# Agent attention with a mixture of experts: 140 stores issued by GpSimd instead of SyncE

## The chip, the cores and the metric

The kernel runs on one core of a Trainium2 chip. The metric is the device time of one execution in microseconds (us); lower is better. The engines of the core are named as the profile names them: PE is TensorE (matrix products; PEld are its weight loads), DVE is VectorE, ACT is ScalarE, POOL is GpSimd, and SP is SyncE, which computes nothing here and only issues DMAs. SPq and POOLq are the instruction queues of SP and POOL.

## The reference

Queries, keys and values are 4 x 11456 x 128, with 49 agents for each of the 4 batches. The agents attend to the keys and gather values; the queries then attend to the 49 agents; the result goes through a top-1 mixture of 8 experts with an inner width of 1024.

```python
def reference(q, k, v, agents, w_gate, w1, w2):
    a2k = softmax(scale * agents @ k.T)          # 49 x 11456 in each batch
    agent_v = a2k @ v                            # 49 x 128
    x = softmax(scale * q @ agents.T) @ agent_v  # 11456 x 128 in each batch
    x = x.reshape(45824, 128)
    logits = x @ w_gate                          # 8 experts
    e = argmax(logits); gate = softmax(logits)[e]
    out = gate * (relu(x @ w1[e]) @ w2[e])
```

## The kernel before

A batch of 11456 tokens is cut into 12 chunks: 11 of 1024 tokens (128 partitions x 8 tokens) and a remainder of 192 (96 x 2). In each batch one expert is applied densely to all tokens, and its product with `agent_v` is folded into the first layer, so that the first layer takes the 49 softmax numerators of a token instead of `x`. Tokens that belong to other experts are gathered, computed in 14 blocks of 128 and written over the dense result at the end, after about 1060 us.

**The dense part** (`experts`) sets the beat. A chunk has two groups of four 128-token tiles (`groups`, 23 in a batch), and a group has 8 steps, one for each 128 columns of the inner width: 184 steps in a batch. In a step TensorE makes two products of 128x512 from the transposed numerators `M` (lines 1186 and 1187), ACT applies the ReLU and rounds to the high half `hh` (line 1192), DVE makes the low half (line 1193), and five steps later (`LAG`) TensorE makes 12 products into `py` (line 1206). After the eighth step `store(g)` multiplies `py` by the gate on DVE into `yo` (line 1219; 3 buffers) and two steps later (`DST`) the 256 KB block goes to `out`.

**Beside it** the attention of the next batch and the rest of this batch's query chunks run, chunk by chunk: load `ld` (SP, line 286), sum of squares (ACT, line 330), split into two 16-bit halves `hl` (ACT line 362, DVE line 364), a DMA transpose to `hT` (SP, line 386, and 390 for the remainder), scores on TensorE (lines 414 to 416). A key chunk then gives `S` (ACT, line 432), later an exponential (ACT, line 481), a running sum `es` (mostly GpSimd, line 491) and products with the values. A query chunk gives `E` (DVE, line 595, subtracts the maximum), `qexp` takes the exponential (ACT, line 600) and stores it to `exps`, a scratch array in device memory, from which the leftover blocks later gather. `esplit` rounds `E` to 16 bits (DVE, line 607) and makes the low part (line 611; on GpSimd for the odd chunks of batches 0 to 2, 18 of 48, else on DVE), `eturn` transposes both to `M` (SP, line 617), and the logits follow on TensorE (line 626). In between, SP loads the experts' weights `wn` (line 905) into the buffers of the keys' `hT`, and ACT takes their sums of squares (line 910).

**The order** of the instructions is written by an event heap: `at(t, f)` puts a function at a step, `after(dt, f)` puts it `dt` steps behind the present one, and a loop at the end takes them out in order of time. A scheduler of the framework may still move instructions on an engine by its own rules when the kernel is built. Each engine then works its list strictly in order, and a DMA is an instruction in the list of the engine that issues it. The stores of the exponentials (48) and of the output (92) are events, and the trace files both under line 1282, from which the loop calls them.

GpSimd's other work: line 491, line 611, the ranks of the leftover tokens (lines 822 to 839), the indirect gathers of the leftover blocks (`fg` and `fx`, line 223) and their indirect stores at the end (line 1088).

## Time and profile before

| what | value |
|---|---|
| median of 3 runs | 1185.75 us (1181.12 to 1194.63) |
| profiled execution | 1183.18 us, of which the span of the instructions is 1181.5 us |
| TensorE busy | 1041.8 us, 88% |
| VectorE busy | 1000.6 us, 85% |
| ScalarE busy | 766.2 us, 65% |
| GpSimd busy | 142.9 us, 12% |
| DMA queues | 62.2% of the 16 engines' span for the queue that SP feeds, 1.1% for the one that GpSimd feeds |

Busy time counts computing instructions, and for GpSimd also the time in which it writes an indirect DMA's work list; it does not count the time in which SP issues a DMA. A share near 90% says that little is left to gain on an engine, and not which wait ends last at a given place; the lists of waits and the order of time say that.

### The profile page before, as it was taken

Reading aid. Unit: us, or ns where it says so; the run is one execution under the profiler, and the core shown is the slowest. Engines: PE = TensorE matmul, PEld = TensorE weight load, DVE = VectorE, ACT = ScalarE, POOL = GpSimd, SP = SyncE. Lnnn points to the kernel's source line nnn. Section 1 sums busy time; section 2 is a strip of 40 time slices with the busy share of each in tenths; the row PEclk is TensorE's granted clock in tenths of the full one; section 3 lists DMA queues with packets and bytes.
Section 4 is the critical chain, followed back from the end, with each engine's and each line's share of the span. In section 5 each row is a group of like instructions: output and inputs, shape, how many; then the busy total and the mean of one; then the engine's idle time right before and its main releaser. Section 6 shows DMA issues by size and latency. Waiting matters only on the chain.

```text
span 1181.5 us, 35109 instructions
## 1 busy us (share of the span) xinstructions
PE 1041.8 (88%) x14308; PEld 828.6 (70%) x14308; DVE 1000.6 (85%) x2512; ACT 766.2 (65%) x1362; POOL 142.9 (12%) x193
## 2 busy tenths in 40 slices
PE   6746989899998899899988989799989889999995
PEld 5625777677775777677776777677767667677885
DVE  7868989697788899698788999697789798899985
ACT  8547876574486786574485887574576556666682
POOL 0200000043000000042100000042000112110123
PEclk9759999999999999899998999999999999899998
DMA  8599899741299899741298899631365545433270
GB/s 325 183 244 222 190 206 232 182 112 46 81 267 222 166 244 219 193 122 40 101 253 224 192 227 215 165 101 49 109 165 117 116 102 132 127 100 125 64 272 14
DMA packets 265669, 190.98 MB, mean 162 GB/s; under 512 B 217513, under 2 KB 230306, under 8 KB 265504
## 3 DMA queue, kind: packets, MB, share of 16 engines
q1 hardware_dynamic: 263648, 185.39, 62.2%
q0 software_dynamic: 1568, 2.25, 1.1%
q8 instruction: 113, 1.85, 0.7%
q10 hardware_dynamic: 288, 1.05, 0.3%
q14 instruction: 52, 0.43, 0.1%
HBM read 99.75 MB, written 36.43 MB: 115 GB/s over the span
## 4 chain that ended last, share of the span: by engine, by line
PE 23%; DVE 16%; DMA 8%; issue 6%; ACT 5%; POOL 2%; SPq 0%; POOLq 0%; ACTq 0%; DVEq 0%
PE py L1206 11%; DVE hh L1193 7%; PE ph L1186 4%; PE ph L1187 4%; DMA M<-mm 3%; ACT hh L1192 2%; DMA wn<-in_moe_w_dram 2%; DVE S L476 1%; POOL out_dram L1088 1%; DMA ld<-in_q_dram 1%; DMA hT<-hl 1%; PE ps_small L504 1%; DVE wsp L1047 1%; ACT jk L330 1%; DVE hl L364 1%
## 5 line engine op out<-in xcount | busy, mean ns | idle before, releaser
L1206 PEld LDWEIGHTS <-hh 128*128 128x128 f16 x8640 | 555.0, 100 | 175.0 <-issue 13.2
L1206 PE MATMUL py<-w2h,hh 128*128 128x128 f16 (+1 forms) x5760 | 614.7, 221 | 3.7 <-DVE E L595 2.4
L1192 ACT ACTIVATE hh<-ph 128x512 f16<-128x512 f32 (+1 forms) x728 | 413.6, 585 | 249.4 <-PE ph L1187 228.9
L1193 DVE SCALAR_TENSOR_TENSOR hh<-ph,hh 128x512 f16<-128x512 f32 (+1 forms) x736 | 481.9, 668 | 86.6 <-ACT hh L1192 83.0
L1206 PE MATMUL py<-w2l,hh 128*128 128x128 f16 (+1 forms) x2880 | 530.2, 221 | 1.4 <-issue 1.2
L1186 PE MATMUL ph<-M,Ah 128*128 128x512 f16 (+1 forms) x736 | 281.9, 384 | 27.2 <-DVE hh L1193 23.5
L1187 PE MATMUL ph<-M,Al 128*128 128x512 f16 (+1 forms) x736 | 281.2, 382 | 0.4 <-issue 0.3
L330 ACT ACTIVATE jk<-ld 128x1024 f16<-128x1024 f32 (+1 forms) x96 | 97.1, 1011 | 25.7 <-DMA ld<-in_q_dram 20.0
L364 DVE SCALAR_TENSOR_TENSOR hl<-ld,mul,hl 128x1024 f16<-128x1024 f32 (+1 forms) x84 | 101.6, 1210 | 3.0 <-ACT hl L362 2.4
L362 ACT ACTIVATE hl<-ld,mul 128x1024 f16<-128x1024 f32 (+1 forms) x84 | 91.5, 1096 | 15.3 <-DVE mul L215 15.0
L1187 PEld LDWEIGHTS <-Al 128*128 128x128 f16 x736 | 72.8, 99 | 34.1 <-issue 32.2
L611 POOL TENSOR_TENSOR mm<-E,mm 128x392 f16<-128x392 f32 (+1 forms) x18 | 19.1, 1060 | 523.6 <-DVE mm L607 491.2
L1186 PEld LDWEIGHTS <-Ah 128*128 128x128 f16 x736 | 74.1, 101 | 10.1 <-issue 7.9
L414 PEld LDWEIGHTS <-hT 128*128 128x128 f16 (+1 forms) x630 | 53.3, 99 | 22.9 <-DMA hT<-hl 20.9
L414 PE MATMUL ps_s<-agh,hT 128*128 128x49 f16 x564 | 53.5, 187 | 16.1 <-DMA hT<-hl 13.9
L1219 DVE TENSOR_TENSOR yo<-py,cs 128x512 f32<-128x512 f32 (+1 forms) x92 | 61.4, 667 | 1.7 <-PE ps_s L626 1.7
L415 PEld LDWEIGHTS <-hT 128*128 128x128 f16 (+1 forms) x630 | 52.4, 99 | 1.4 <-issue 1.0
L415 PE MATMUL ps_s<-agl,hT 128*128 128x49 f16 x564 | 53.0, 186 | 0.0
L416 PE MATMUL ps_s<-agh,hT 128*128 128x49 f16 x564 | 52.8, 186 | 0.0
L416 PEld LDWEIGHTS <-hT 128*128 128x128 f16 (+1 forms) x630 | 52.0, 99 | 0.3 <-issue 0.3
L491 POOL TENSOR_TENSOR es<-es,S 128x392 f32<-128x392 f32 (+1 forms) x39 | 42.5, 1090 | 23.3 <-ACT S L481 16.6
L600 ACT ACTIVATE E<-E,ln,div 128x392 f32<-128x392 f32 (+1 forms) x48 | 33.3, 693 | 12.3 <-DVE E L595 8.6
(303 smaller groups left out, 1304.3 us busy)
## 6 DMA issues: line engine op xcount, KB each, us to landing
ld<-in_k_dram SPq DMA_DIRECT2D x44, 512.0 KB
ld<-in_v_dram SPq DMA_DIRECT2D x44, 512.0 KB
ld<-in_q_dram SPq DMA_DIRECT2D x44, 512.0 KB
out_dram<-yo SPq DMA_DIRECT2D x88, 256.0 KB
w1e<-in_moe_w_dram SPq DMA_DIRECT2D x17, 512.0 KB
w2e<-in_moe_w_dram SPq DMA_DIRECT2D x17, 512.0 KB
exps<-E SPq DMA_DIRECT2D x44, 196.0 KB
wn<-in_moe_w_dram SPq DMA_DIRECT2D x16, 512.0 KB
```

What stands on the lines that cost most here:

```text
L330: nc.scalar.activation(jk[:p, :t * D], x[:p, :t, :].rearrange("p t d -> p (t d)"), AF.Square, accum_out=ss[:p])
L362: nc.scalar.activation(hi[:p, :t, :], x[:p, :t, :], AF.Copy, scale=m)
L364: nc.vector.scalar_tensor_tensor(lo[:p, :t, :], x[:p, :t, :], m, hi[:p, :t, :], op0=ALU.mult, op1=ALU.subtract)
L414: nc.tensor.matmul(o, x[:, 0, i, :p], AG["h"], start=True, stop=False)
L415: nc.tensor.matmul(o, x[:, 0, i, :p], AG["l"], start=False, stop=False)
L416: nc.tensor.matmul(o, x[:, 1, i, :p], AG["h"], start=False, stop=True)
L1186: nc.tensor.matmul(ph[:, :nn], st['Ah'][:, f, :], m, start=True, stop=False)
L1187: nc.tensor.matmul(ph[:, :nn], st['Al'][:, f, :], m, start=False, stop=True)
L1192: nc.scalar.activation(hh[:, 0, :nn], ph[:, :nn], AF.Relu)
L1193: nc.vector.scalar_tensor_tensor(hh[:, 1, :nn], ph[:, :nn], 0.0, hh[:, 0, :nn], op0=ALU.max, op1=ALU.subtract)
L1206: mm_ = lambda l, r, **k: nc.tensor.matmul(o, l, r, skip_group_check=True, **k)
L1219: nc.vector.tensor_tensor(yo[:p, :n, :], py[:p, :n * D].rearrange("p (i d) -> p i d", d=D), cs.unsqueeze(2).broadcast_to([p, n, D]), op=AL ...
```

## The change

Both stores are issued by GpSimd instead of SyncE. Nothing else in the source is changed: sources, destinations, sizes and the steps at which the events stand are the same.

```diff
             nc.scalar.activation(ev, ev, AF.Exp, scale=SC["q", c][1][:p, :1], bias=ln32[:p])
-            after(DEX, nc.sync.dma_start, chunk_view(exps[b * N:(b + 1) * N, :], c), ev)
+            after(DEX, nc.gpsimd.dma_start, chunk_view(exps[b * N:(b + 1) * N, :], c), ev)
...
             ov = out[b * N + t0:b * N + t0 + p * t, :].rearrange("(p t) d -> p t d", t=t)
-            after(DST, nc.sync.dma_start, ov[:, h:h + n, :], yo[:p, :n, :])
+            after(DST, nc.gpsimd.dma_start, ov[:, h:h + n, :], yo[:p, :n, :])
```

On GpSimd's list, where the odd chunks of batch 1 are split (`mm_142` is the 16-bit buffer that the odd chunks use, `E` the numerators), these rows stand before:

```order
L833 MEMSET cp 128x8
L611 TENSOR_TENSOR mm_142<-E,mm_142 128x8x49 x5
L488 COPY es<-S 128x392
L491 TENSOR_TENSOR es<-es,S 128x392 x10
L491 TENSOR_TENSOR es<-es,S 96x98
L611 TENSOR_TENSOR mm_142<-E,mm_142 96x2x49
```

and now, from the same place:

```order
L1282 DMA exps<-E 128x392
L611 TENSOR_TENSOR mm_142<-E,mm_142 128x8x49
L1282 DMA out_dram<-yo 96x256
L1282 DMA exps<-E 128x392
L1282 DMA out_dram<-yo 128x512
L1282 DMA exps<-E 128x392
L611 TENSOR_TENSOR mm_142<-E,mm_142 128x8x49
L1282 DMA out_dram<-yo 128x512 x2
L1282 DMA exps<-E 128x392
L1282 DMA out_dram<-yo 128x512
L1282 DMA exps<-E 128x392
```

The store of a chunk's exponentials now stands directly ahead of the low part (line 611) of the same or the next chunk, and output stores stand between the others. Each DMA that GpSimd issues also waits for the eighth one before it.

On SP's list, near the end of batch 1's queries, where the first weights are loaded (`wn`; `mm_141` and `mm_142` are the 16-bit buffers of the even and odd chunks), these rows stand before:

```order
L1282 DMA exps<-E 128x392
L1282 DMA out_dram<-yo 128x512
L617 DMA_TRANSPOSE M<-mm_141 128x8x128
L1282 DMA out_dram<-yo 128x512
L905 DMA wn<-in_moe_w_dram 128x1024
L390 DMA_TRANSPOSE hT<-hl 128x2x96 x2
L905 DMA wn<-in_moe_w_dram 128x1024
L1282 DMA exps<-E 128x392
L617 DMA_TRANSPOSE M<-mm_142 128x8x128
L905 DMA wn<-in_moe_w_dram 128x1024
L1282 DMA out_dram<-yo 128x512
L905 DMA wn<-in_moe_w_dram 128x1024 x3
```

and now:

```order
L617 DMA_TRANSPOSE M<-mm_141 128x8x128
L905 DMA wn<-in_moe_w_dram 128x1024
L390 DMA_TRANSPOSE hT<-hl 128x2x96 x2
L905 DMA wn<-in_moe_w_dram 128x1024
L617 DMA_TRANSPOSE M<-mm_142 128x8x128
L905 DMA wn<-in_moe_w_dram 128x1024 x4
```

The stores are gone from between the transposes and the weight loads, and the other rows keep their order.

On TensorE's list the order is nearly the same but for batch 0 and the end of batch 3. At one place in batch 0 (`hT_2480` is a transposed query chunk, `ps_s_2633` its scores, `ph` and `py` the two layers of the dense part) these rows stand before:

```order
L1187 MATMUL ph_2462<-M_1606,Al_1136 128x512
L1186 LDWEIGHTS Ah_1135
L1186 MATMUL ph_2482<-M_1606,Ah_1135 128x512
L1187 LDWEIGHTS Al_1136
L1187 MATMUL ph_2482<-M_1606,Al_1136 128x512
L414 LDWEIGHTS hT_2480
L414 MATMUL ps_s_2633<-agh_1230,hT_2480 128x49
L415 LDWEIGHTS hT_2480
L415 MATMUL ps_s_2633<-agl_1231,hT_2480 128x49
L416 LDWEIGHTS hT_2480
L416 MATMUL ps_s_2633<-agh_1230,hT_2480 128x49
```

and now:

```order
L1206 MATMUL py_2620<-w2h_1169,hh_2507 128x128
L1206 LDWEIGHTS hh_2507
L1206 MATMUL py_2620<-w2l_1170,hh_2507 128x128
L1206 LDWEIGHTS hh_2507
L1206 MATMUL py_2620<-w2h_1169,hh_2507 128x128
L414 LDWEIGHTS hT_2480
L414 MATMUL ps_s_2633<-agh_1230,hT_2480 128x49
L415 LDWEIGHTS hT_2480
L415 MATMUL ps_s_2633<-agl_1231,hT_2480 128x49
L416 LDWEIGHTS hT_2480
L416 MATMUL ps_s_2633<-agh_1230,hT_2480 128x49
```

The scores of that chunk stand six steps of the dense part later, behind products of the second layer. The scores and logits of three earlier chunks in batch 0 likewise stand two steps later.

## Rows read from the trace of the kernel before

**Rows 1.** The page's first and second parts: busy time of each engine with its share of the span, and the clock that TensorE was granted, in 40 equal slices of the span, in tenths of full speed.

```profile
PE 1041.8 (88%) x14308; PEld 828.6 (70%) x14308; DVE 1000.6 (85%) x2512; ACT 766.2 (65%) x1362; POOL 142.9 (12%) x193
...
PEclk9759999999999999899998999999999999899998
```

**Rows 2.** The page's parts on the queues (packets, megabytes, share of the 16 DMA engines' span) and on the chain of work that ended last, by engine and by line.

```profile
q1 hardware_dynamic: 263648, 185.39, 62.2%
q0 software_dynamic: 1568, 2.25, 1.1%
...
PE 23%; DVE 16%; DMA 8%; issue 6%; ACT 5%; POOL 2%; SPq 0%; POOLq 0%; ACTq 0%; DVEq 0%
PE py L1206 11%; DVE hh L1193 7%; PE ph L1186 4%; PE ph L1187 4%; DMA M<-mm 3%; ACT hh L1192 2%; DMA wn<-in_moe_w_dram 2%; DVE S L476 1%; POOL out_dram L1088 1%; DMA ld<-in_q_dram 1%; DMA hT<-hl 1%; PE ps_small L504 1%; DVE wsp L1047 1%; ACT jk L330 1%; DVE hl L364 1%
```

**Rows 3.** What TensorE waited for between 70 and 1060 us (engine, its tile and line, what it waited for: us in total, times, longest).

```profile
PE ps_s L626 <- DMA M<-mm: 20.2, 13, 4.4
PE ps_s L414 <- DMA hT<-hl: 13.9, 7, 3.7
```

**Rows 4.** What ScalarE waited for over the whole span (columns as above).

```profile
ACT jk L910 <- DMA wn<-in_moe_w_dram: 27.6, 11, 5.6
ACT jk L330 <- DMA ld<-in_q_dram: 20.0, 5, 9.7
```

**Rows 5.** SyncE's instruction queue (SPq): what it waited for at line 1282 over the span; then the duration of the instructions of line 1282, under which the trace files what the event loop starts (ns, shortest/median/longest, first and last start).

```profile
SPq L1282 <- DVE yo L1219: 177.5, 35, 10.9
...
SPq L1282 <- ACT E L600: 71.7, 24, 8.4
...
L1282 SPq DMA_DIRECT2D out_dram<-yo x92: 332/366/1763, 115.9 to 1126.8; - x92
L1282 SPq DMA_DIRECT2D exps<-E x48: 319/331/1162, 73.8 to 1025.5; - x48
```

**Rows 6.** SyncE's queue in order of time at two places (start us, duration us, line, operation, out<-in).

```profile
428.42 0.38 SPq L1282 DMA_DIRECT2D exps<-E  x1
428.89 0.38 SPq L1282 DMA_DIRECT2D out_dram<-yo  x1
429.37 2.14 SPq L617 DMA_TRANSPOSE M<-mm  x1
...
615.54 0.33 SPq L1282 DMA_DIRECT2D exps<-E  x1
615.97 3.38 SPq L386 DMA_TRANSPOSE hT<-hl  x1
```

**Rows 7.** SyncE's queue from 477 to 480 us, and what ScalarE waited for at line 910 between 476 and 500 us.

```profile
477.08 0.53 SPq L1282 DMA_DIRECT2D exps<-E  x1
477.71 1.30 SPq L617 DMA_TRANSPOSE M<-mm  x1
479.10 0.53 SPq L1282 DMA_DIRECT2D out_dram<-yo  x1
479.72 0.39 SPq L905 DMA_DIRECT2D wn<-in_moe_w_dram  x1
...
ACT jk L910 <- DMA wn<-in_moe_w_dram: 9.9, 4, 5.6
```

**Rows 8.** SyncE's queue from 935.3 to 936.2 us.

```profile
935.34 0.37 SPq L1282 DMA_DIRECT2D exps<-E  x1
935.75 0.43 SPq L286 DMA_DIRECT2D ld<-in_q_dram  x1
```

**Rows 9.** GpSimd's groups by line (count | busy us, mean ns of one | idle us just before, and what ended it), and three of its instructions in order of time (start us, duration us, [idle before, what ended it]).

```profile
L611 POOL TENSOR_TENSOR mm<-E,mm 128x392 f16<-128x392 f32 (+1 forms) x18 | 19.1, 1060 | 523.6 <-DVE mm L607 491.2 <-DVE hb L211 32.4
L1088 POOL DMA_INDIRECT out_dram<-yb,fti x14 | 18.6, 1330 | 41.3 <-DVE yb L1082 37.0 <-issue 4.3
...
L223 POOL DMA_INDIRECT fx<-exps,ftr x14 | 14.3, 1021 | 79.1 <-ACT hh L1192 21.8 <-DVE gs L662 21.1 <-DVE ftr L985 20.5
...
426.83 1.31 POOL L611 TENSOR_TENSOR mm<-E,mm 128x392 f16<-128x392 f32 x1 [34.92 <-DVE mm L607]
...
1116.20 1.00 POOL L223 DMA_INDIRECT fx<-exps,ftr  x1 [0.30 <-issue]
...
1137.51 1.96 POOL L1088 DMA_INDIRECT out_dram<-yb,fti  x1 [2.05 <-DVE yb L1082]
```

**Rows 10.** The operations on one chunk's tile E between 687.5 and 694 us (operation, duration in ns, first and last start).

```profile
L600 ACT ACTIVATE E<-E,ln,div x1: 732/732/732, 688.3 to 688.3; 128x392 f32<-128x392 f32 x1
L607 DVE CAST mm<-E x1: 370/370/370, 689.1 to 689.1; 128x392 f16<-128x392 f32 x1
L611 POOL TENSOR_TENSOR mm<-E,mm x1: 1876/1876/1876, 689.5 to 689.5; 128x392 f16<-128x392 f32 x1
```

**Rows 11.** TensorE at 151 us in order of time; what it waited for at line 626 between 95 and 118 us; and three stretches (window, its length, busy time of each engine with the number of instructions, granted clock, DMA share, GB/s).

```profile
150.96 0.22 PE L414 MATMUL ps_s<-agh,hT 128*128 128x49 f16 x1 [3.66 <-DMA hT<-hl]
...
PE ps_s L626 <- DMA M<-mm: 4.0, 1, 4.0
...
113.30:120.00 6.70, 4.69 (x59) 4.15 (x60) 3.98 (x12) 2.86 (x4) 0.00 (x0) 0.50 1.05 310
147.30:150.90 3.60, 0.00 (x0) 0.00 (x0) 3.51 (x8) 2.12 (x5) 0.00 (x0) 0.99 1.06 269
150.90:154.30 3.40, 3.35 (x35) 2.25 (x36) 0.53 (x1) 1.19 (x2) 0.00 (x0) 0.50 1.23 228
```

## The prediction, written before the result was known

> **What bounds the kernel now.** I read the busy times first, then the chain of waits, and then, for each engine on that chain, what it waited for. TensorE is busy 88% of the 1181.5 us span and VectorE 85%; GpSimd is busy 12% [rows 1]. The chain says the same in another way: most of it is TensorE and VectorE, 8% is DMA, and SyncE's own queue is 0% [rows 2]. So no single engine is at its end, and what a change of issuing engine can win is among the DMA waits. They are listed by engine. TensorE waits 20.2 us for the transposed numerators M and 13.9 us for transposed inputs hT between 70 and 1060 us [rows 3]; ScalarE waits 27.6 us for the expert weights whose norms it takes and 20.0 us for query loads [rows 4]. All of these transfers are issued by SyncE, in the same list as the 140 stores. Nobody waits for a store itself but the reuse of its buffer.
>
> The stores cost SyncE little: 92 at a median of 366 ns and 48 at 331 ns, some 50 us in 1181.5 [rows 5]. The 177.5 and 71.7 us that the list stood at a store until VectorE or ScalarE had made the data [rows 5] look like the prize, since everything behind such a store is held up. In the order of time they are nearly all stretches in which the next instruction of the list has to wait for the same or later work anyway, or is another store. What the stores cost others has therefore to be counted place by place.
>
> **The change part by part.** The measure is the profiled execution, 1183.18 us, 1.7 us more than its span; it lies 2.6 us under the median of 1185.75.
>
> *Stores taken from ahead of a transpose.* A store that stands directly ahead delays what follows by its own time and a gap: 615.97 minus 615.54 is 0.43 us for one, and 429.37 minus 428.42 is 0.95 us for two [rows 6]. Most transposes for which TensorE waits stand behind another transpose of 2 to 3.4 us, which stays, or are issued as soon as their source is ready. I find three places (near 352, 615 and 672 us) where TensorE waits, a single store is directly ahead, and the low part was not made on GpSimd: 3 x 0.43 = **1.3 us** less. The bound is none of it if the DMA engines and not the issue set the landing.
>
> *Stores taken from ahead of the weight loads.* At 477 us two stores stand among what precedes the weight loads; 479.72 minus 477.08 is 2.64 us, of which the transpose M takes 1.30 and a gap 0.09, so the stores take 1.25 us. ScalarE waits 9.9 us there for the weights, and TensorE waits for ScalarE [rows 7]. The same sequence comes once more, near 740 us: 2 x 1.25 = **2.5 us** less, 0 to 3.75 (a third place near 205 us).
>
> *Stores taken from ahead of a query load.* One, near 935 us: 935.75 minus 935.34, **0.4 us** less [rows 8].
>
> *Stores put on GpSimd's list.* GpSimd did no plain store before. The nearest rows are its indirect DMAs, which also move 128 rows each: the gathers of `exps` take 1.02 us in the mean (1.00 in most, 0.30 between two), and the block stores at the end up to 1.96 us [rows 9]. I take 1.02 + 0.30 = 1.32 us, because the gathers run while VectorE works on the dense part as it would around the new stores; the upper end is 1.96 + 0.30 = 2.26, the lower end nothing. 140 x 1.32 = 185 us on an engine with 12% busy is no load by itself. What counts is what is queued behind: the low part of line 611. In GpSimd's new order the store of the same chunk's exponentials is directly ahead of it, and starts when ScalarE ends its exponential, at 688.3 + 0.73 = 689.03 in the chunk shown; the low part started at 689.53, when VectorE's rounding had ended [rows 10]. With the store ahead it starts at 689.03 + 1.32 = 690.35, 0.8 us later, and the transpose, the logits and the first layer follow it. 18 of 48 chunks go this way [rows 9], and matched with TensorE's 13 waits at line 626 [rows 3] five or six of them reach TensorE; for the others there is slack. 6 x 0.8 = 4.9 us more. At two of these places (428 and 692 us) the transpose was also held up by two stores in SyncE's list, which goes: 2 x 0.95 = 1.9 less [rows 6]. Net **3.0 us** more, from 1.9 less (the DMA hidden) to 8.7 more (6 x 1.76 - 1.9 at 2.26 us). The other work of GpSimd (`es`, ranks, gathers) has more slack: its idle stretch before a low part is 35 us in the row at 426.83 [rows 9].
>
> The Trainium skill, page "SBUF — State Buffer", section "SBUF: two separate sides", speaks against the change: a DMA issued by GpSimd has its descriptors written by GpSimd, which certain VectorE operations lock out of a shared port, and it advises to issue from the ACT or SP queue. It puts 620 ns alone against 3100 ns beside a VectorE copy; by the larger figure the term would be 6 x 2.9 - 1.9, an estimate of some 15 us more. The gathers at 1.0 us, with VectorE busy 85% of the span, speak against such a lock being usual here; the 1.96 us rows leave it open.
>
> *The order in batch 0.* Freed from the stores, the scheduler puts one chunk's scores six steps later. In the trace of before TensorE stood 3.66 us for their hT, and in the 3.4 us behind that its granted clock was 0.50, the lower of its two levels (1.2 against 2.4 GHz), after a stretch in which it did nothing [rows 11]. With six steps of dense work ahead the wait is gone and the 3.4 us at half clock are worth 1.7: 5.4 us less. An earlier wait for M, 4.0 us, is followed by 6.7 us at 0.50 [rows 11]; its logits move two steps, which may take away up to 4.0 + 3.4 = 7.4 more, or nothing, since the scores that come before them move as well. I take **5.4 us** less, 0 to 12.8. In the end phase the stores are past or nobody waits behind them, and the order there costs nothing that I see.
>
> The sum is -1.3 - 2.5 - 0.4 + 3.0 - 5.4 = -6.6: 1176.6 us for an execution like the profiled one, 1179.1 on the median. I forecast 1178.
>
> **The rivals.** *The stores were hidden anyway.* The transfers that TensorE waits for are late because of transposes and a busy queue (62.2% of the 16 engines' span [rows 2]), not because of a third of a microsecond of issue. The small gains and the GpSimd loss cancel, -1.3 - 2.5 - 0.4 + 3.0 = -1.2, and the new order in batch 0 only moves its wait to the next chunk's load: 1182.0, on the median 1184.6, say 1185. For it: SyncE's 0% on the chain. Against it: a wait of 3.66 us whose place in the list has really changed. The Trainium skill, page "DMA: Bandwidth & Descriptors", section "Issuing engines are not separate DMA queues", says that DMAs from different engines run on the same 16 engines and that spreading the issue saves sequencer time alone; by that rule it is this rival rather than the next. No run here shows it yet.
>
> *Loads and transposes overtake the stores in the DMA engines.* The stores carry 45824 x (512 + 196) bytes = 32.4 MB of the 185.39 MB in SyncE's queue, 17.5%; GpSimd's goes through a queue of its own with 1.1% [rows 2]. If what SyncE issues no longer stands behind store packets, the waits on transfers shrink by that share: 17.5% of 20.2 + 13.9 + 27.6 + 20.0 = 81.7 us [rows 3, 4] is 14.3 us in place of the 4.2 of the first three terms. 1183.2 - 14.3 + 3.0 - 5.4 = 1166.5, on the median 1169. Against it: the DMA share of 1.05 to 1.23 where TensorE stands [rows 11], at which the stores take the same bandwidth from whichever queue.
>
> *Slower: GpSimd becomes the late link between exponential and M.* If VectorE's work stretches the writing of a store's work list as the 1.96 us rows may show, every low part starts 1.76 us later, chunks with less slack than that reach TensorE as well, and the output stores that fall ahead of two of the low parts add 2.26 each. With 12 of the 18 on the path: 12 x 1.76 + 2 x 2.26 - 1.9 = 23.7 us. 1183.2 - 4.2 + 23.7 - 5.4 = 1197.3, on the median 1200. It decides from about 2 us per store on; at 1.3 us it is the 3 us of the sum. Line 611 itself takes 1.06 us in the mean, but 1.31 at 426.83 and 1.88 at 689.5 for the same work [rows 9, 10], which shows that GpSimd is slowed at times.
>
> **How the numbers follow.** About 1% is what a measurement of this kernel can tell from no change: 1173.9 to 1197.6. Forecast 0.38, of which 0.06 lies below 1173.9, where the batch-0 term comes out near its upper end; hidden anyway 0.20; overtaking 0.24; GpSimd late 0.18. So faster 0.30, same 0.52, slower 0.18. The range goes from 1162, which is the overtaking with most of the 12.8 us of batch 0, to 1200, the slower rival's middle; some 0.08 is left out below and 0.09 above.
>
> **What would show it.** Right: the wait for hT at 151 us is gone from TensorE's list and the clock there stays up; ScalarE's wait for weights falls by 2 to 4 us; GpSimd's stores take about 1.0 us each and stand some 140 to 185 us busy; the low part starts about 0.8 us later behind ScalarE's exponential. Overtaking: all the DMA waits of lines 626, 414, 910 and 330 shrink together with no change of the issue times. Slower: stores of 2 us and more on GpSimd, and line 626 waiting on M more often than 13 times, always in odd chunks. The forecast would be wrong above all if the scheduler's new order in batch 0 meets loads that are later than before, or if GpSimd waits for an output block with a low part queued behind it.

## The result, and the profile after

The changed kernel has a median of 1192.34 us (15 runs, 1186.27 to 1199.86), the kernel before 1187.28 us on the same chip (15 runs): a ratio of 1.0071, with an interval of 1.0049 to 1.0093. One execution of the kernel before took 2059.2 us and is left out of the ratio; the others took 1181.12 to 1194.63 us. The losses in this text are such a ratio less 1, times the median of the kernel before, here 8.4 us; the two medians themselves lie 5.1 us apart, and a second series of both kernels (after_again below) gives 9.5 us by the ratio and 7.1 by the medians. So the kernel is slower, by some 5 to 11 us. The measured time lies within 1% and inside the range that was given, but the forecast was a gain of 7 us, so its sum failed in sign. The profiled execution took 1192.34 us with a span of 1190.3.

The page of the changed kernel: busy times, the granted clock in 40 slices, the two queues, and the first line of the chain.

```profile
PE 1043.0 (88%) x14308; PEld 829.7 (70%) x14308; DVE 1003.0 (84%) x2512; ACT 766.7 (64%) x1362; POOL 218.4 (18%) x333
...
PEclk9758998989999999999998999899999999899998
...
q1 hardware_dynamic: 243744, 152.94, 53.8%
q0 software_dynamic: 11744, 34.71, 8.6%
...
DVE 15%; PE 11%; issue 5%; DMA 4%; ACT 2%; POOL 1%; SPq 0%; POOLq 0%; ACTq 0%; DVEq 0%
```

Against [rows 1, 2] the change did what it says: 32.4 MB went from SyncE's queue to GpSimd's, and GpSimd is busy 75.5 us longer. The other engines do the same work in nearly the same time (VectorE, with 2.4 us more, differs most). The chain breaks off early and is of little use here.

What TensorE waited for between 70 and 1060 us after, the rows for transposes (`ps_y` and `ps_s` are two buffers for the same products):

```profile
PE ps_s L626 <- DMA M<-mm: 24.3, 11, 4.9
...
PE ps_s L414 <- DMA hT<-hl: 7.0, 5, 2.5
...
PE ps_y L414 <- DMA hT<-hl: 4.6, 1, 4.6
...
PE ps_y L626 <- DMA M<-mm: 3.7, 1, 3.7
```

and the rows of before for the second buffer, which [rows 3] leave out:

```profile
PE ps_y L414 <- DMA hT<-hl: 2.8, 2, 2.2
...
PE ps_y L626 <- DMA M<-mm: 0.9, 1, 0.9
```

What ScalarE waited for over the span after:

```profile
ACT jk L910 <- DMA wn<-in_moe_w_dram: 27.1, 11, 6.8
ACT jk L330 <- DMA ld<-in_q_dram: 24.7, 7, 13.2
```

With both buffers counted the waits for hT fell from 16.7 to 11.6 us and those for M grew from 21.1 to 28.0. Beside [rows 4], those for weights stayed and those for queries grew by 4.7. Of the waits that the prediction laid to SyncE's list (M, weights, queries) none became clearly smaller.

A part of the loss is not in any of these lists. Line 1351 is the closing code behind the kernel's own instructions. On GpSimd it has three DRAIN instructions; the row gives the shortest, median and longest in ns, and behind the longest come 0.8 us of short instructions and the end. Before:

```profile
L1351 POOLq DRAIN  x3: 40/109/4707, 1176.0 to 1181.2; - x3
```

After:

```profile
L1351 POOLq DRAIN  x3: 40/115/7327, 1182.2 to 1190.1; - x3
```

The closing drain takes 7.33 us where it took 4.71: 2.6 of the 8.8 us by which the span grew. In the order of time, from the starts of the 736 instructions of line 1193 in both traces, the rest is nearly all lost by the end of batch 0: the changed kernel lies 5.6 us behind at step 128 of batch 0 (of 184) and 6.0 at the end of batch 3's steps. Of the 5.6, 2.6 are there at the first step, behind a wait for hT that was 2.17 us before and is 4.61 now:

```profile
79.22 0.22 PE L414 MATMUL ps_y<-agh,hT 128*128 128x49 f16 x1 [2.17 <-DMA hT<-hl]
```

```profile
83.16 0.22 PE L414 MATMUL ps_y<-agh,hT 128*128 128x49 f16 x1 [4.61 <-DMA hT<-hl]
```

This is one execution of each kernel. In the second trace of the changed kernel (after_again, on another chip) the steps lie 6.3 us behind the same trace of before at step 128, and 1.1 us ahead at the end of batch 3's, so where the rest is lost isn't settled by it.

### The profile page after: what moved, and what is told of

Same layout as the page of the kernel before. It is cut to its first block, busy times and chain, and to the rows that moved or that the text cites. A ratio compares the mean times of both kernels' runs of the same rounds, so it can differ in the third digit from the quotient of the medians.

```text
span 1190.3 us, 35149 instructions
## 1 busy us (share of the span) xinstructions
PE 1043.0 (88%) x14308; PEld 829.7 (70%) x14308; DVE 1003.0 (84%) x2512; ACT 766.7 (64%) x1362; POOL 218.4 (18%) x333
## 5 line engine op out<-in xcount | busy, mean ns | idle before, releaser
L1206 PEld LDWEIGHTS <-hh 128*128 128x128 f16 x8640 | 557.2, 100 | 176.5 <-issue 13.5
L1282 POOL DMA_DIRECT2D out_dram<-yo x92 | 50.6, 550 | 501.7 <-DVE yo L1219 366.4
L1187 PEld LDWEIGHTS <-Al 128*128 128x128 f16 x736 | 73.1, 99 | 32.4 <-issue 31.3
L1282 POOL DMA_DIRECT2D exps<-E x48 | 26.9, 559 | 286.0 <-ACT E L600 242.2
```

The source lines that it names most:

```text
L1187: nc.tensor.matmul(ph[:, :nn], st['Al'][:, f, :], m, start=False, stop=True)
L1206: mm_ = lambda l, r, **k: nc.tensor.matmul(o, l, r, skip_group_check=True, **k)
L1282: f(*a)
```

## The experiments

Each ratio is against the kernel before on the same chip, in the same series of runs, with its 95% interval. Chips differ (the kernel before took 1175 to 1187 us on them), so ratios are compared and not times. Diffs show only what differs from the kernel before.

### Is it the order in batch 0?

The new order in batch 0 is brought about by one store alone, that of the first chunk's exponentials. So three kernels: that store alone on GpSimd; the same with the eighth chunk's M put ahead of the hT that had overtaken it; and all stores but two.

**first_store**

```diff
+            after(DEX, (nc.gpsimd if b == 0 and c == 0 else nc.sync).dma_start, chunk_view(exps[b * N:(b + 1) * N, :], c), ev)
```

> The kernel before with one store moved to GpSimd: that of the exponentials of the first chunk of batch 0; the other 139 stay on SyncE. With that one store the scheduler already writes batch 0 in nearly the order of the changed kernel (transposes M and hT change places on SyncE's list twice, the scores move six steps on TensorE's). ORDER-AND-DRAIN THEORY: the loss of batch 0 comes from this order and not from GpSimd, so the dense steps at the end of batch 0 lie 5 to 6 us later than before, a wait of TensorE of 3.5 to 4 us for M stands near 198 us, the closing drain of GpSimd stays at 4.7 us, and the span is 5 to 6.5 us longer (about 1187.5). LATE-LINK THEORY (the loss is what the stores do on GpSimd's list, chunk by chunk over the run): no difference to before beyond 1 us (1181.5), since GpSimd carries one store.

**first_store_m7**, beside the edit above:

```diff
-            at(base + t + ql_ + 3, esplit, c)
+            at(base + t + ql_ + (2 if first and c == 7 else 3), esplit, c)
```

> As the run with the first store alone, and in the eighth chunk of batch 0 the low part is written one step earlier, which puts its transpose M ahead of the transpose hT on SyncE's list again, where it stands in the kernel before; TensorE's order is unchanged against that run. ORDER-AND-DRAIN THEORY: TensorE's wait for M near 198 us and the lower clock behind it go, 5 to 6 us, while the 3.9 us gained near 150 us stay; the end of batch 0 is within 1.5 us of before and the span 1180 to 1183. If the loss of batch 0 has another cause than this change of places, the span stays that of the run with the first store alone (about 1187.5). LATE-LINK THEORY: 1181.5 for both runs.

**all_but_two**

```diff
+            after(DEX, (nc.sync if b == 0 and c < 2 else nc.gpsimd).dma_start, chunk_view(exps[b * N:(b + 1) * N, :], c), ev)
+            after(DST, nc.gpsimd.dma_start, ov[:, h:h + n, :], yo[:p, :n, :])
```

> The changed kernel with the exponentials' stores of the first two chunks of batch 0 left on SyncE; the other 138 stores are on GpSimd. TensorE's and SyncE's transposes then stand in batch 0 in the order of before. ORDER-AND-DRAIN THEORY: the dense steps lie within 1 us of before up to the end of batch 3; the closing drain of GpSimd takes 4.71 + 138 x 0.019 = 7.3 us, so the span is 2 to 3.5 us longer than before (about 1184.3). LATE-LINK THEORY: the low parts of 16 odd chunks still wait for a store, so nearly the whole 8.8 us of the changed kernel remains (about 1190).

Measured: first_store 1.0012 [0.9989, 1.0034], first_store_m7 1.0003 [0.9975, 1.0031], all_but_two 1.0088 [1.0057, 1.0118]. The new order alone costs nothing that can be told from zero, and the kernel without it (all_but_two) loses as much as the changed one. The order is not the cause, and it is not the gain of 5.4 us of the forecast either.

### Is it the bytes, or the number of GpSimd's DMAs?

**tiny138** leaves the stores with SyncE and adds 138 stores of one row of 64 bytes on GpSimd.

```diff
+            [after(DST + 0.5, nc.gpsimd.dma_start, tiny[j:j + 1, :], ones[:1, :16]) for j in range(2 * (b * NG + g), 2 * (b * NG + g) + 2 * (b > 0))]
```

> The kernel before, all its 140 stores on SyncE, with 138 small stores of one row of 64 bytes added on GpSimd in batches 1 to 3, two behind each output store, into a scratch array that nobody reads. It measures what lengthens the closing drain of GpSimd. ORDER-AND-DRAIN THEORY: if the drain goes by the number of DMAs that GpSimd issued (182 in the changed kernel against 42), it takes 7.3 us here (180 DMAs) and the span is 2 to 3.5 us longer than before; if it goes by rows or bytes moved, it stays at 4.7 us and the span at 1181.5. LATE-LINK THEORY: GpSimd is held as often as in the changed kernel ahead of its low parts in batches 1 and 2, so the dense part is 2 us or more later before the end is reached.

Measured: 1.0605 [1.0555, 1.0656]. It tells nothing of the question, because the design was wrong. The added stores depend on no other work, and the scheduler moved them all to the head of GpSimd's list, so that GpSimd's other work stood behind them. The last of them starts at 168 us, and SyncE's first output store at 186.5 us, where it had been at 115.9 [rows 5]:

```profile
L1282 POOL DMA_DIRECT2D tiny<-ones x138: 484/484/736, 2.9 to 168.2; - x138
...
L1282 SPq DMA_DIRECT2D out_dram<-yo x92: 332/353/1442, 186.5 to 1188.8; - x92
```

**quarter_sync** and **quarter_gpsimd** store only the first of the four tiles of each output block; the rest of the output is left out. The first is the kernel before with that edit, the second the changed kernel.

```diff
+            after(DST, nc.sync.dma_start, ov[:, h:h + 1, :], yo[:p, :1, :])
```

> The kernel before, but each output store writes only the first of its four 128-token tiles (64 KB in place of 256 KB, as many DMAs and as many rows in each); the rest of the output is left out. All stores on SyncE. It is the partner of the run with quarter stores on GpSimd and has to be read against it. Both theories: less traffic, so the waits for transposes and loads shrink and the time is 0.5 to 1.5% below before. CONTENTION THEORY (a store on GpSimd goes out beside the transposes that SyncE issues at the same moment, and these land later; SyncE's own list kept them apart): the gap between the two quarter runs closes to the closing drain of GpSimd, about 2.5 us or 0.2%. LATE-LINK THEORY (GpSimd's list holds up the low parts): the gap stays as wide as between the changed kernel and before, 0.7%.

> The changed kernel, but each output store writes only the first of its four 128-token tiles; the rest of the output is left out. TensorE's and SyncE's lists are those of the changed kernel. CONTENTION THEORY: TensorE's wait for M in batches 1 and 2, 16.8 us in the changed kernel against 12.6 before, falls to 12.6 or less, the time from a transpose's issue to the logits in the chunks that TensorE waits for falls by 1 us or more (6.6 us at the first chunk of batch 2 in the changed kernel), and the time is within 0.35% of the quarter stores on SyncE. LATE-LINK THEORY: the waits for M stay at 16 us or more and the time is 0.5 to 0.8% above the quarter stores on SyncE.

Measured: 0.9894 [0.9854, 0.9934] and 0.9994 [0.9967, 1.0021]. With 17.5 MB less to write the distance between the two issuing engines is still 1.0%. So three quarters of the output's bytes in GpSimd's queue are not what costs; the bytes of the exponentials are the same in both.

### Which of the stores?

**exps_only** moves the 48 stores of exponentials, **out_only** the 92 of the output.

```diff
+            after(DEX, nc.gpsimd.dma_start, chunk_view(exps[b * N:(b + 1) * N, :], c), ev)
```

> Half of the change: only the 48 stores of exponentials on GpSimd, 196 KB each; the output stores stay on SyncE. CONTENTION THEORY: these are 28% of the stores' bytes, so 28% of some 5.5 us, and a third of the longer drain, 0.9 us: 2 to 3 us over before (1.002). LATE-LINK THEORY: it is this store that stands directly ahead of the low parts, so nearly all of the loss is here: 6 to 8 us (1.006).

```diff
+            after(DST, nc.gpsimd.dma_start, ov[:, h:h + n, :], yo[:p, :n, :])
```

> The other half: only the 92 output stores on GpSimd, 256 KB each; the exponentials' stores stay on SyncE. CONTENTION THEORY: 72% of the bytes, so some 4 us, and two thirds of the longer drain, 1.7 us: 5 to 7 us over before (1.005). LATE-LINK THEORY: only two low parts have an output store directly ahead, so 2 us with the drain (1.0015).

Measured: 1.0092 [1.0059, 1.0126] and 1.0034 [1.0002, 1.0066]. Either half loses, and the half with fewer stores loses more. Most of that difference is in its closing drain:

```profile
L1351 POOLq DRAIN  x3: 40/109/8634, 1173.0 to 1182.2; - x3
```

In exps_only the drain takes 8.63 us, in out_only 3.55. With 42 indirect DMAs in every kernel, GpSimd issues 42 DMAs before, 43 with first_store, 90 with exps_only, 134 with out_only and 182 after. The drain is 4.71, 4.80, 8.63, 3.55 and 7.33 us: about 1.3 + 0.081 us for each DMA, and somewhere between 90 and 134 it drops by about 8.7 and starts to rise again. From here on this was a rule to be tested. The row of out_only:

```profile
L1351 POOLq DRAIN  x3: 40/115/3549, 1177.3 to 1181.4; - x3
```

### The closing drain as a sawtooth

**out_69** (output stores of batches 1 to 3), **out_58** (the same less the last 11), **b0_on_sync** (all but the 35 stores of batch 0) and **b0_on_gpsimd** (those 35 alone) vary number and place.

```diff
+            after(DST, (nc.gpsimd if b else nc.sync).dma_start, ov[:, h:h + n, :], yo[:p, :n, :])
```

> Only the 69 output stores of batches 1 to 3 on GpSimd, everything else on SyncE; 111 DMAs by GpSimd in all. SAWTOOTH-AND-BATCH-0 THEORY: GpSimd's closing drain grows by 0.08 us with each DMA and falls back after some 107 (4.71 us after 42 DMAs, 4.80 after 43, 8.63 after 90, 3.55 after 134, 7.33 after 182); after 111 it is 1.7 us, 3 us less than before. The rest of the loss arises in batch 0, which is untouched here. So the time is 2 to 4 us below before (0.997). LATE-LINK THEORY: 69 of 140 stores, no gain from the drain that would outweigh them: 2 to 4 us above before (1.003). A drain that simply grows with the DMAs would be 6.0 us.

```diff
+            after(DST, (nc.gpsimd if b and (b < 3 or g < 12) else nc.sync).dma_start, ov[:, h:h + n, :], yo[:p, :n, :])
```

> As the run with 69 output stores, but the last 11 of batch 3 stay on SyncE: 58 output stores on GpSimd, 100 DMAs by GpSimd in all. SAWTOOTH-AND-BATCH-0 THEORY: the closing drain is near the top of its sawtooth, 1.3 + 100 x 0.081 = 9.4 us, and the time is 7.7 us above the run with 69 stores and 4 to 5 us above before (1.004). LATE-LINK THEORY, or a drain that simply grows: within 1 us of the run with 69 stores, slightly less.

```diff
+            after(DEX, (nc.gpsimd if b else nc.sync).dma_start, chunk_view(exps[b * N:(b + 1) * N, :], c), ev)
+            after(DST, (nc.gpsimd if b else nc.sync).dma_start, ov[:, h:h + n, :], yo[:p, :n, :])
```

> The changed kernel with the 35 stores of batch 0 left on SyncE; 105 stores on GpSimd, 147 DMAs by GpSimd in all. SAWTOOTH-AND-BATCH-0 THEORY: the drain is 1.3 + (147 - 107) x 0.081 = 4.5 us, as before, and batch 0 is as before, so the time is that of before within 2 us (0.999 to 1.002). LATE-LINK THEORY: 12 of the 18 low parts behind a store, three quarters of the loss, 1.005 to 1.006.

```diff
+            after(DEX, (nc.sync if b else nc.gpsimd).dma_start, chunk_view(exps[b * N:(b + 1) * N, :], c), ev)
+            after(DST, (nc.sync if b else nc.gpsimd).dma_start, ov[:, h:h + n, :], yo[:p, :n, :])
```

> The other part: only the 35 stores of batch 0 on GpSimd, 105 on SyncE; 77 DMAs by GpSimd in all. SAWTOOTH-AND-BATCH-0 THEORY: the drain is 1.3 + 77 x 0.081 = 7.5 us, 2.8 more than before, and the loss of batch 0 is all there, 4 to 6 us: 7 to 9 us above before (1.006 to 1.0075). LATE-LINK THEORY: one quarter of the loss, 2 us (1.002).

Measured: out_69 1.0089 [1.0058, 1.0120], out_58 1.0092 [1.0056, 1.0128], b0_on_sync 0.9995 [0.9968, 1.0022], b0_on_gpsimd 1.0081 [1.0049, 1.0114]. The drains came out at 9.45 us for 100 DMAs, 4.56 for 147 and 7.57 for 77, as the rule says. For 111 (out_69) it was 10.35 and not past the drop, so the drop lies between 111 and 134. The rows of out_69 and out_58:

```profile
L1351 POOLq DRAIN  x3: 40/115/10349, 1186.0 to 1196.9; - x3
L1351 POOLq DRAIN  x3: 40/115/9454, 1185.5 to 1195.5; - x3
```

and of b0_on_sync:

```profile
L1351 POOLq DRAIN  x3: 44/115/4557, 1176.4 to 1181.6; - x3
```

### Small stores, with SyncE's list as it was

The rule was then tried on the time itself, with stores that move no work: **dose54** and **dose96** leave the 140 stores with SyncE and add 54 and 96 stores of 128 rows of 64 bytes on GpSimd, made from `yo` so that they keep their place. In the same series **b0_at_147** takes the changed kernel to 147 DMAs by giving the last 35 output stores back, and **after_again** is the changed kernel once more.

```diff
+            [after(DST + 0.5, nc.gpsimd.dma_start, tiny[j * P:j * P + p, :], yo[:p, 0, :16]) for j in range(2 * (b * NG + g), 2 * (b * NG + g) + 1 * (b < 3 and g >= 5))]
```

> The kernel before, all its 140 stores on SyncE and its list unchanged, with 54 small stores (128 rows of 64 bytes) added on GpSimd, one behind every output store from the sixth group on in batches 0 to 2, into a scratch array. 96 DMAs by GpSimd in all, so its closing drain is 1.3 + 96 x 0.081 = 9.1 us, 4.4 more than before; nothing else of the stores is moved. DRAIN THEORY (what lies between the changed kernel and before is mostly the drain, and a kernel pays for it at least what the profile shows): 4 to 9 us above before (1.004 to 1.0075). BATCH-0 THEORY (drain and lists of batch 0 each take their part): 4 to 5 us (1.004). CONTENTION OR LATE-LINK THEORY: within 2 us of before.

dose96 has `2 * (b < 3 and g >= 7)` in the last place.

> As the run with 54 small stores, but two behind every output store from the eighth group on: 96 small stores, 138 DMAs by GpSimd in all, past the point at which the drain falls back: 3.9 us, 0.8 less than before. DRAIN THEORY and BATCH-0 THEORY: within 2 us of before (0.998 to 1.001) and 4 us or more below the run with 54, though GpSimd issues 42 DMAs more. LATE-LINK THEORY: GpSimd is held up more often than with 54, so 1 us or more above that run.

```diff
+            after(DEX, nc.gpsimd.dma_start, chunk_view(exps[b * N:(b + 1) * N, :], c), ev)
+            after(DST, (nc.sync if b == 3 or (b == 2 and g >= 11) else nc.gpsimd).dma_start, ov[:, h:h + n, :], yo[:p, :n, :])
```

> The changed kernel with the last 35 output stores (12 groups of batch 2 and all 23 of batch 3) left on SyncE, batch 0 as in the changed kernel: as many stores on GpSimd (105) and as many DMAs (147) as in the run that left batch 0 on SyncE, so the same drain of 4.5 us. It tells the part of batch 0 from that of the drain. BATCH-0 THEORY: 4 to 6 us above before (1.0035 to 1.005). DRAIN THEORY: within 2 us of before (1.000).

> The changed kernel once more, beside the three other runs on the same chip, for its ratio and a second trace. All theories: 1.005 to 1.009, a drain of 7.3 us; the dense steps at the end of batch 0 later than in the trace of before by 1 to 8 us, and how much the place of the waits repeats shows what of the first trace was chance.

Measured: dose54 1.0104 [1.0070, 1.0138], dose96 1.0055 [1.0021, 1.0088], b0_at_147 1.0051 [1.0015, 1.0087], after_again 1.0081 [1.0052, 1.0111]. The drain of dose54:

```profile
L1351 POOLq DRAIN  x3: 45/109/9124, 1173.2 to 1182.8; - x3
```

and of dose96, with 42 DMAs more:

```profile
L1351 POOLq DRAIN  x3: 45/109/3729, 1183.2 to 1187.5; - x3
```

The drains differ by 5.4 us and the times by 5.7 (12.2 against 6.5), the kernel with fewer DMAs being the slower one. The same holds of out_69 against out_only, in two series (10.5 and 4.0 us, drains 10.35 and 3.55). With some 4 us on each loss a single pair would not prove it, but both agree with the drain in sign and size, and in every trace it is the last long thing that the program does. after_again against b0_at_147, in one series, agrees too: 3.5 us of time for 2.8 of drain. But dose96, whose drain is shorter than before, is still 6.5 us slower.

**dose_b0** and **dose_b12** then put 32 small stores into batch 0 and 64 into batches 1 and 2, to see where that rest is lost (`2 * (b == 0 and g >= 7)` and `2 * (0 < b < 3 and g >= 7)` in the last place).

> The kernel before with the 32 small stores of batch 0 alone that the run with 96 had there (two behind every output store from the eighth group on); 74 DMAs by GpSimd in all, a drain of 1.3 + 74 x 0.081 = 7.3 us, 2.6 over before. BATCH-0 THEORY (what remains beside the drain, some 6.5 us in nearly all runs with stores of GpSimd in batch 0, arises there): 2.6 + 6.5 = 9 us above before (1.0077). SPREAD THEORY (each store of GpSimd costs the same wherever it stands): 2.6 + a third of 7.5 = 5 us (1.0043).

> The kernel before with the other 64 small stores, those of batches 1 and 2; 106 DMAs by GpSimd in all, a drain of 1.3 + 106 x 0.081 = 9.9 us, 5.2 over before. BATCH-0 THEORY: the drain alone, 5 us above before (1.0045), and 4 us below the run with 32 in batch 0. SPREAD THEORY: 5.2 + two thirds of 7.5 = 10 us (1.0087), and 5 us above that run.

Measured: 1.0115 [1.0068, 1.0162] and 1.0119 [1.0076, 1.0163]. Both lose, so neither "only in batch 0" nor "by their number" holds. For the drain this pair is no witness: 2.9 us more of it in dose_b12 show as 0.5 us, well inside the intervals.

### All runs beside each other

n is the number of DMAs that GpSimd issues. "Loss" is the ratio less 1, times the median of before in that series. "Rest" is the loss less what the drain grew by. "Waits" are TensorE's for M and hT between 70 and 1060 us in the profiled execution, both buffers together. "Clock" is the mean granted clock over the timed executions, less that of before in the same series (not kept for the first comparison). tiny138 and the two quarter runs, told above, are not in the table.

| kernel | n | loss us | drain us | rest us | waits us | clock |
|---|---|---|---|---|---|---|
| before | 42 | 0 | 4.71 | 0 | 37.8 | 0 |
| after | 182 | 8.4 | 7.33 | 5.8 | 39.6 | - |
| after_again | 182 | 9.5 | 7.33 | 6.9 | 43.0 | -0.0020 |
| all_but_two | 180 | 10.3 | 7.17 | 7.9 | 44.5 | -0.0035 |
| b0_at_147 | 147 | 6.0 | 4.55 | 6.2 | 45.6 | -0.0022 |
| b0_on_sync | 147 | -0.6 | 4.56 | -0.4 | 37.0 | +0.0011 |
| out_only | 134 | 4.0 | 3.55 | 5.2 | 45.9 | -0.0022 |
| out_69 | 111 | 10.5 | 10.35 | 4.9 | 43.4 | -0.0045 |
| out_58 | 100 | 10.9 | 9.45 | 6.2 | 41.2 | -0.0045 |
| exps_only | 90 | 10.8 | 8.63 | 6.9 | 36.6 | -0.0044 |
| b0_on_gpsimd | 77 | 9.6 | 7.57 | 6.7 | 44.3 | -0.0044 |
| first_store | 43 | 1.4 | 4.80 | 1.3 | 37.0 | -0.0012 |
| first_store_m7 | 43 | 0.4 | 4.80 | 0.3 | 36.6 | -0.0004 |
| dose54 | 96 | 12.2 | 9.12 | 7.8 | 41.1 | -0.0031 |
| dose96 | 138 | 6.5 | 3.73 | 7.5 | 41.2 | -0.0010 |
| dose_b0 | 74 | 13.5 | 7.02 | 11.2 | 40.0 | -0.0053 |
| dose_b12 | 106 | 14.0 | 9.94 | 8.8 | 41.8 | -0.0068 |

With intervals of 3 to 6 us either way on each loss, the rest is 5 to 11 us wherever GpSimd issues 32 plain stores or more among the dense part, but for b0_on_sync, and it does not rise with their number. Where there is a rest, the mean clock is lower, and TensorE in most cases stands longer for its transposes, but not in all: exps_only has a rest of 6.9 us with shorter waits than before, and between the two quarter runs, which lie 11.8 us apart (9.2 beyond the drain), the waits are 35.6 us with SyncE's stores and 36.4 with GpSimd's, while the clock differs by 0.0043. How far the clock could go is an estimate from the table: its fall times a span of 1185 us is what it costs if TensorE sets the pace throughout. That is some 5.3 us at 0.0045, but 1.2 in dose96, whose rest is 7.5.

## Why the prediction was wrong, point by point

Three steps of the sum failed: it had no term for the closing stage; it counted the order in batch 0 as 5.4 us won, where the runs show none; and it took 4.2 us for stores taken out of SyncE's list, where the waits did not shrink. Beyond these a loss remains whose cause is not known.

**The closing stage** was left out of the sum. It is 2.6 us of the 8.4: the drains in the two traces differ by that, and the pairs of runs with longer and shorter drains show that the time goes with them, as far as their intervals tell.

**Stores ahead of transposes (-1.3) and of weight loads (-2.5), and of a query load (-0.4): not won.** At the two places followed in order of time, 353 and 615 us, the transpose was issued sooner behind its source, by 2.2 and 2.8 us and not the 0.43 of the sum, but TensorE could use it only 0.6 and 0.2 us sooner behind that source, and waited longer for it. The place at 615 us of [rows 6] shows it. Before, M stood behind the store and the 3.38 us of hT and was issued at 619.45, 2.8 us after its low part had ended (line 611 on VectorE, 616.09 + 0.56), and TensorE waited 4.4 us for it, the longest of [rows 3]:

```profile
619.45 2.26 SPq L617 DMA_TRANSPOSE M<-mm  x1
```

After, SyncE issues its loads ahead without stopping at the store, and M at 619.52, 0.03 us after the low part (618.93 + 0.56):

```profile
612.18 0.38 SPq L286 DMA_DIRECT2D ld<-in_k_dram  x1
612.61 0.42 SPq L286 DMA_DIRECT2D ld<-in_q_dram  x1
613.09 1.97 SPq L286 DMA_DIRECT2D ld<-in_k_dram  x2
615.15 0.52 SPq L286 DMA_DIRECT2D ld<-in_q_dram  x1
619.52 1.50 SPq L617 DMA_TRANSPOSE M<-mm  x1
```

TensorE stands 4.9 us for it instead of 4.4 (the longest of its waits for M after, in the rows above): what was won in the issue was nearly all lost in the landing, which by TensorE's first use of it came 4.0 us after the issue before and 6.6 after:

```profile
623.46 0.38 PE L626 MATMUL ps_s<-Gs,M 128*128 128x18 f16 x8 [4.43 <-DMA M<-mm]
```

```profile
626.14 0.38 PE L626 MATMUL ps_s<-Gs,M 128*128 128x18 f16 x8 [4.92 <-DMA M<-mm]
```

From 617 to 624 us the two traces read (length, busy times, granted clock, DMA share, GB/s), before

```profile
617.00:624.00 7.00, 2.57 (x52) 2.23 (x49) 4.29 (x10) 2.39 (x7) 0.00 (x0) 0.85 1.17 166
```

and after

```profile
617.00:624.00 7.00, 4.22 (x99) 4.07 (x96) 6.39 (x14) 5.22 (x14) 1.01 (x2) 1.00 1.25 353
```

so the transpose now runs beside twice the bytes a second. That these bytes are what delays it is likely but was not tested. The first chunk of batch 1 goes the same way: M is issued 2.2 us sooner behind its low part, its landing takes 1.7 us longer, and TensorE waits 3.5 us where it waited 2.8. The bound that the prediction named for this term ("none of it if the DMA engines and not the issue set the landing") was the answer here. ScalarE's wait for the weights near 480 us [rows 7] was 8.4 us after and 11.1 in after_again, against 9.9 before, so no gain shows there either. The Trainium skill, page "DMA: Bandwidth & Descriptors", section "Issuing engines are not separate DMA queues", says that spreading the issue saves sequencer time alone; here 50 us of that were saved and bought nothing that the time shows.

**GpSimd's list (+3.0): the late starts are there, the price was wrong.** The durations of the new stores:

```profile
L1282 POOL DMA_DIRECT2D out_dram<-yo x92: 526/542/596, 116.2 to 1133.0; - x92
L1282 POOL DMA_DIRECT2D exps<-E x48: 526/542/819, 71.5 to 1032.6; - x48
```

A plain store takes 0.54 us of GpSimd, not the 1.02 + 0.30 taken from the gathers. Eight of the 18 low parts start 0.32 to 0.92 us behind the rounding where they had started 0.08 behind it; the worst has two stores ahead of it (the rounding ended at 431.39):

```profile
431.23 0.54 POOL L1282 DMA_DIRECT2D exps<-E  x1 [12.15 <-ACT E L600]
431.75 0.54 POOL L1282 DMA_DIRECT2D out_dram<-yo  x1
432.31 0.92 POOL L611 TENSOR_TENSOR mm<-E,mm 128x392 f16<-128x392 f32 x1
```

Together that is 3.9 us. The runs show no price for it that can be told from zero: b0_on_sync has the late starts of batches 1 and 2 as the changed kernel has them (six of 0.33 to 0.92 us) and loses nothing, while in out_69 no low part of these batches starts more than 0.23 us behind the rounding, and its rest is 4.9 us. The place of the worst one in b0_on_sync, and the same chunk in out_69:

```profile
427.55 0.54 POOL L1282 DMA_DIRECT2D exps<-E  x1 [11.79 <-ACT E L600]
428.08 0.54 POOL L1282 DMA_DIRECT2D out_dram<-yo  x1
428.64 0.93 POOL L611 TENSOR_TENSOR mm<-E,mm 128x392 f16<-128x392 f32 x1
```

```profile
434.69 0.54 POOL L1282 DMA_DIRECT2D out_dram<-yo  x1 [14.36 <-DVE yo L1219]
435.25 1.16 POOL L611 TENSOR_TENSOR mm<-E,mm 128x392 f16<-128x392 f32 x1
```

The slower rival, which needed 2 us for a store, did not come about: it was right on the side and wrong on the cause. The Trainium skill, page "SBUF — State Buffer", section "SBUF: two separate sides", gives 620 ns for such a DMA alone and 3100 ns beside a VectorE copy; the longest of 140 here, with VectorE busy 84%, took 819 ns of GpSimd's time, so no run here shows the larger figure.

**The order in batch 0 (-5.4): won and lost again.** The wait of 3.66 us at 151 us [rows 11] went as forecast and the clock stayed up behind it. But in the new order the eighth chunk's M is issued behind an hT of 5.07 us:

```profile
188.62 5.07 SPq L386 DMA_TRANSPOSE hT<-hl  x1
193.79 1.27 SPq L617 DMA_TRANSPOSE M<-mm  x1
```

and TensorE stands for it and has the lower clock afterwards. The row at 198.62 in order of time:

```profile
198.62 0.38 PE L626 MATMUL ps_y<-Gs,M 128*128 128x18 f16 x8 [3.68 <-DMA M<-mm]
```

and the windows of both places after (window, length, busy times, granted clock, DMA share, GB/s):

```profile
147.30:150.90 3.60, 2.69 (x40) 1.53 (x37) 3.56 (x9) 3.60 (x5) 0.00 (x0) 1.00 0.45 156
150.90:154.30 3.40, 2.83 (x48) 2.65 (x48) 3.40 (x8) 3.40 (x7) 1.13 (x3) 1.00 1.10 215
194.90:198.60 3.70, 0.03 (x1) 0.00 (x0) 3.19 (x10) 2.03 (x3) 0.00 (x0) 0.90 1.19 209
198.60:203.00 4.40, 4.38 (x36) 3.29 (x37) 1.34 (x4) 1.19 (x2) 0.00 (x0) 0.50 0.93 248
```

In the order of time the changed kernel, 2.6 us behind at batch 0's first step, was 1.4 ahead at step 40 and gave back 5.4 between steps 72 and 76. The prediction had said that the new order might meet transfers that are later than before, and put no number on it. first_store, which has nearly this order with one store on GpSimd, measured the term: +1.4 us with an interval of -1.3 to +4.0, in place of -5.4. In its trace the same wait for M is 1.50 us and not 3.68, so the price of this place is not the order's alone.

**Overtaking (1169) fell.** SyncE's queue lost 17.5% of its bytes and the waits of line 626 grew.

**The balance.** From -6.6 to +8.4 are 15.0 us: 2.6 of the drain, 6.8 of the order in batch 0 (by first_store, 2.6 either way), and 5.6 of all the rest, forecast as -1.2 and found at +4.4.

**What stays open.** 5.8 us of the 8.4 (4.9 to 7.9 in most other kernels) are lost outside the drain. Some traces show transposes that take longer to land, and TensorE waits for M 28.0 us after and 31.7 in after_again instead of 21.1, both buffers counted. They do not show why, and in exps_only and the quarter runs there is a rest without longer waits. It isn't most of the output's bytes (quarter_gpsimd), nor a store's time on GpSimd's list ahead of the low parts (out_69 has a rest without it), nor SyncE's relief alone, with its earlier loads, since the dose kernels keep SyncE's stores and lose as well. It isn't the number of GpSimd's DMAs, nor their being in batch 0 alone. And b0_on_sync, with 105 stores on GpSimd, loses nothing, while out_69 with 69 of these 105 does (rests of -0.4 and 4.9 us in one series). The lower clock can be cause or consequence: in the rows at 151 and 198 us it fell behind a wait. One trace of a kernel also settles little at this size, since executions of the changed kernel differ by up to 14 us and its waits for transposes were 39.6 and 43.0 us in two traces. A run of single stores moved one at a time around a fixed chunk would be needed. No version that writes the whole output beat the kernel before beyond its interval.

## What to carry to other kernels

When DMAs are moved to another issuing engine, look at the closing stage as well as at the lists: work that no engine's busy time counts can be on the end of the path. Taking a third of a microsecond from ahead of a transfer pays only where the issue and not the landing sets the wait, and the trace tells which: compare the end of the source's last write, the issue, and the first use. A term that rests on one wait in one trace, made by an order that a scheduler writes, should be followed to the next such wait in the new list before it is counted.

## What the runs showed of the hardware that was not expected

- The closing drain of GpSimd grows by 0.081 us for each DMA that it has issued in the program (4.71 us at 42, 8.63 at 90, 10.35 at 111) and is 8.7 us shorter past a number between 111 and 134 (3.55 at 134, 4.56 at 147, 7.33 at 182). What is done in that time, no run shows. The small stores fit a little less well (7.02 at 74 in dose_b0, where the line gives 7.3), and the one-row stores of tiny138 count less: 6.10 us at 180.
- A plain store of 128 rows costs GpSimd 0.54 to 0.56 us in the median whatever its row length: 64 bytes (0.540 in dose54), 1568 bytes (0.542 after, 0.562 in exps_only) or 2048 bytes (0.542 after). Its indirect gathers take 1.02 [rows 9].
- In the kernels that have all or nearly all of the 140 stores on GpSimd the time outside the span is 1.9 to 2.0 us in the mean of the timed executions, elsewhere 1.7.
